# One branch per pair on TensorE, a merged last routing group, and work of the expert stage moved in its queues

## The chip, the cores and the metric

The kernel runs on one core of one Trainium2 chip. The metric is the device time of one execution in microseconds (us), as the median of several runs. PE is TensorE's matmul, PEld its weight load, DVE VectorE, ACT ScalarE, POOL GpSimd, SP SyncE (it issues most of the DMAs). A q behind an engine's name means its sequencer, which waits, loads registers and branches.

## The reference

Random-feature attention, followed by a mixture of experts with one expert per token:

```python
def phi(x):
    proj = np.einsum('bhsd,md->bhsm', x, omega)
    sq = np.sum(x * x, axis=-1, keepdims=True) / 2.0
    h = proj - sq
    h = h - np.max(h, axis=-1, keepdims=True)
    return np.exp(h) / np.sqrt(m)
...
kv = np.einsum('bhsm,bhsd->bhmd', k_p, v)
z = np.sum(k_p, axis=2)
num = np.einsum('bhsm,bhmd->bhsd', q_p, kv)
den = np.einsum('bhsm,bhm->bhs', q_p, z)[..., None] + 1e-06
...
logits = x @ w_gate
expert_idx = np.argmax(logits, axis=1)
...
    h = np.maximum(xe @ w1[e], 0.0)
    ye = h @ w2[e]
    out[mask] = gate_w[mask, None] * ye
```

q, k and v are 8 x 8 x 576 x 64 float32, omega is 128 x 64. The 4608 tokens have 512 columns; there are 8 experts, w1 is 8 x 512 x 1024 and w2 is 8 x 1024 x 512. The expert of a token is known only once its row of the attention is.

## The kernel before, in words

**Attention.** `Attention.run` goes through 72 units (a batch's remainder rows, then its eight heads), a software pipeline written out by hand: in each round of the loop the next unit is transposed, this one projected, the one before exponentiated, and so on, and each engine takes its instructions in just the order in which the code issues them. `unit_sum` adds up k' over the rows on POOL (tile `ks`), and two units later `unit_df` multiplies it on PE. `finish` writes a batch's rows to DRAM (`token_rows`).

**Routing.** While attention runs, `Routing.some` pops small steps from a queue in between. `rest` queues a group of steps (`group`): the argmax of a token's logits, its one-hot row `OH`, its rank among the tokens of its expert (`rr`, many short matmuls), the gate weight. Batches 0 to 5 are grouped in pairs (9 columns), batch 6 and batch 7 alone (4 and 5 columns). For every column two 128 x 128 tiles `rt_RH` are made (`rh`, L600): those that are queued go to POOL a few per round (`row`), those of the last group are the "tail" that `slots` makes, four of them on ACT in two steps each and the rest on DVE. `slots` then counts the tokens of each expert, and one matmul over all `rt_RH` gives the list of tokens in expert order, cut in tiles of 128 (`idx`). `plan` turns the counts into flags that the engines load into registers.

**Experts.** Two tiles of 128 tokens make a pair. Weights and activations are split in a high and a low float32r part, and each product is three matmuls (L990 to L992). Pair 0 is an exception: it is chosen from the first four batches alone, gathered in the last rounds of the attention (`ahead`), and multiplied in plain float32 (`products0`, `l20`), so that PE has work while `slots` runs. From pair 1 on a pair goes so: `gather` (POOL, indirect DMA), `move` (SP: rows to DRAM and back into `xq`, blocked), `xtrans` (DVE: two stream transposes and the low part `xb`; ACT: the high part), `two` (PE: 96 matmuls of layer 1, L927; ACT `relu`, DVE `hlow`), `l2` (PE: 24 matmuls for each of the two tiles), `store`. A pair whose second tile is empty takes `one` in place of `two`, and its second `l2` is skipped: two branches per pair on PE, both by the flag in row 4, `If(full)` in `step` and `when` for `l2(t, 1)`. `change` splits new weights (`split`, L46 on DVE and L52 on ACT) where the expert changes.

The order in a step is the code's: `step(t)` issues the gather of t+2, layer 1 of t, then `following` (that is `begin(t + 1)`: `xtrans(t + 1)`, `move(t + 2)`, the split of new w1), then layer 2 of t, then its branch for the second tile. For this data the expert stage has pairs 1 to 19; two of them have one tile, and both are followed by a change of expert.

```python
    def begin(self, t):
        self.xtrans(t)
        if t + 1 < NPR:
            self.move(t + 1)
        self.change(t, 1)
```

The tiles of `slots` (`f_cnt` and on) come from a pool that opens after the attention and lies on memory that the attention's tiles held.

## Time and profile before

| | us |
|---|---|
| median of 3 runs | 708.39 (707.14 to 709.19) |
| the profiled execution | 707.54 |
| its span, first to last instruction | 705.8 |
| PE busy in the span | 677.3 (96%) |
| PEld / DVE / ACT / POOL busy | 610.2 / 373.2 / 356.6 / 269.0 |
| mean granted clock of TensorE | 0.990 |

The page shows PE busy in nearly every slice, attention to about 246 us, the list of slots to 262 us, then the experts to 692 us. Where one engine is busy throughout, the time follows from the work on that engine and from the few places in which it stands still; these are found in the order of time, engine by engine. Column "idle before" of a timeline row, in brackets, says how long the engine stood still before it and what ended that.

### The profile page before, as it was taken

The numbers are of one execution on the slowest core, as the hardware profiler recorded it, in microseconds if no ns is written. First come the engines' busy times: TensorE is split into PE (matmuls) and PEld (weight loads), VectorE is DVE, ScalarE is ACT, GpSimd is POOL, SyncE is SP. The second block draws the span as 40 slices with busy tenths as digits, with TensorE's granted clock in tenths as the row PEclk, the third lists the DMA queues.
The fourth block names the chain that finished last, engine by engine and source line by source line (L and its number), as shares of the span: only waits on it lengthen the run. The fifth ranks groups of instructions, "written<-read, shape, count | busy, mean of one in ns | idle before, by whom it ended". The sixth has DMA issues, their size and how long they took to land. (4 is left out here: it accounts for less than half of the span.)

```text
span 705.8 us, 19757 instructions
## 1 busy us (share of the span) xinstructions
PE 677.3 (96%) x7590; PEld 610.2 (86%) x7590; DVE 373.2 (53%) x748; ACT 356.6 (51%) x1083; POOL 269.0 (38%) x487
## 2 busy tenths in 40 slices
PE   6999999999999899999999999999999999999992
PEld 5999999999899885999889998899888889998891
DVE  4788888888888776531233272331493376312310
ACT  4999999999999624421222162221272244212210
POOL 5544557877887663212202213112222023122010
PEclk9999999999999999999999999999999999999997
DMA  6872754826672124843223256323257338331200
GB/s 180 245 239 73 233 161 120 266 77 199 214 283 72 33 70 175 253 143 122 76 80 106 92 173 237 107 69 113 91 182 236 102 107 319 109 108 61 77 19 20
DMA packets 92430, 99.56 MB, mean 141 GB/s; under 512 B 28942, under 2 KB 72974, under 8 KB 91664
## 3 DMA queue, kind: packets, MB, share of 16 engines
q1 hardware_dynamic: 85744, 78.91, 35.3%
q0 software_dynamic: 6560, 19.03, 8.0%
q8 instruction: 72, 1.18, 0.7%
q14 instruction: 54, 0.44, 0.2%
HBM read 71.06 MB, written 29.51 MB: 142 GB/s over the span
## 5 line engine op out<-in xcount | busy, mean ns | idle before, releaser
L927 PEld LDWEIGHTS p<-xb,w1p 128*128 128x128 f32 x1632 | 194.7, 188 | 5.7 <-ACT w1p L52 2.9
L927 PE MATMUL p<-xb,w1p 128*128 128x256 f32 x1632 | 196.6, 280 | 2.3 <-ACT w1p L52 2.0
L998 POOL DMA_INDIRECT out_dram<-ys,idx x38 | 41.0, 1080 | 323.2 <-ACT ys L997 206.4
L983 DVE SCALAR_TENSOR_TENSOR hl<-p,hh 128x512 fp32r<-128x512 f32 x68 | 46.5, 691 | 220.5 <-ACT hh L979 210.3
L990 PE MATMUL p<-w2p,hh 128*128 128x512 f32 x288 | 113.9, 396 | 0.0
L991 PE MATMUL p<-w2p,hh 128*128 128x512 f32 x288 | 113.8, 395 | 0.0
L992 PE MATMUL p<-w2p,hl 128*128 128x512 f32 x288 | 113.8, 395 | 0.0
L979 ACT ACTIVATE hh<-p 128x512 fp32r<-128x512 f32 x68 | 40.3, 597 | 127.7 <-PE p L927 123.6
L997 ACT ACTIVATE ys<-p,gt 128x512 f32<-128x512 f32 x38 | 26.2, 688 | 116.8 <-PE p L992 93.4
L172 DVE TENSOR_REDUCE mx<-pp 128x8 f32<-128x1024 f32 x64 | 78.0, 1219 | 9.4 <-PE pp L166 8.7
L180 ACT ACTIVATE qp<-pp,mx 128x128 f32<-128x128 f32 x256 | 76.8, 431 | 0.0
L180 ACT ACTIVATE kp<-pp,mx 128x128 f32<-128x128 f32 x256 | 73.7, 381 | 4.3 <-DVE de L264 1.3
L166 PE MATMUL pp<-omt,th 64*128 64x128 f32 x1024 | 72.1, 281 | 0.0
L992 PEld LDWEIGHTS p<-w2p,hl 128*128 128x128 f32 x288 | 54.1, 188 | 13.2
L991 PEld LDWEIGHTS p<-w2p,hh 128*128 128x128 f32 x288 | 54.1, 188 | 12.2
L990 PEld LDWEIGHTS p<-w2p,hh 128*128 128x128 f32 x288 | 54.1, 188 | 12.2
L166 PEld LDWEIGHTS pp<-omt,th 64*128 64x128 f32 x1024 | 63.5, 191 | 0.0
L192 POOL TENSOR_TENSOR k<-kp 128x256 f32<-128x256 f32 x64 | 46.5, 726 | 26.1 <-ACT kp L180 21.4
L255 PE MATMUL nu<-kva,qt 128*64 128x73 f32 x1008 | 46.6, 235 | 0.0
L157 DVE COPY th<-tr 128x512 f32<-128x512 f32 x63 | 43.3, 687 | 6.1 <-PE tr L151 4.2
L224 ACT COPY qt<-t 128x512 f32<-128x512 f32 x64 | 41.6, 650 | 2.6 <-PE t L151 2.2
L255 PEld LDWEIGHTS nu<-kva,qt 128*64 128x64 f32 x1008 | 37.1, 137 | 4.2
(379 smaller groups left out, 1063.0 us busy)
## 6 DMA issues: line engine op xcount, KB each, us to landing
w1s<-in_moe_w_dram SPq DMA_DIRECT2D x5, 2048.0 KB
w2s<-in_moe_w_dram SPq DMA_DIRECT2D x5, 2048.0 KB
xq<-pair_rows SPq DMA_DIRECT2D x76, 128.0 KB
v<-in_v_dram SPq DMA_DIRECT2D x32, 256.0 KB
token_rows<-x SPq DMA_DIRECT2D x8, 1024.0 KB
k<-in_k_dram SPq DMA_DIRECT2D x31, 256.0 KB
q<-in_q_dram SPq DMA_DIRECT2D x31, 256.0 KB
pair_rows<-xg SPq DMA_DIRECT2D x10, 512.0 KB
```

What stands on the lines that cost most here:

```text
L157: self.nc.vector.tensor_copy(t.rearrange("p n (a t) -> p a n t", a=2), s[("tr", h)])
L166: nc.tensor.matmul(o[:, a, n, :], t[r, n, :], self.om[r], start=True, stop=True)
L172: self.nc.vector.tensor_reduce(out=mx, in_=s[("pp", h)], axis=AX.X, op=ALU.max, negate=True)
L180: self.nc.scalar.activation(o[:, j, :], p[:, a, 2 * n + i, :], AF.Exp, bias=mx[:, a, 2 * n + i:2 * n + i + 1])
L192: nc.gpsimd.tensor_tensor(out=k2, in0=kp[:, :2, :], in1=kp[:, 2:, :], op=ALU.add)
L224: self.nc.scalar.copy(qt.rearrange("p n (a t) -> p a n t", a=2), s[("t2", h)])
L255: nc.tensor.matmul(o[r, j, :], qt[:, j, r], kva[:, h if h >= 0 else 2 * j + a, :], start=True, stop=True)
L927: return [lambda w=w, x=x, c=c, n=n: self.nc.tensor.matmul(o, w[:, c, f], x[:, c, :], start=n == 0, stop=n == len(ops) - 1) for n, (w, x, ...
L983: self.nc.vector.scalar_tensor_tensor(out=b, in0=self.p_1[g], scalar=0.0, in1=a.bitcast(F32), op0=ALU.max, op1=ALU.subtract)
L990: nc.tensor.matmul(p, h[:, c, k], self.w2h[:, c, :], start=c == 0, stop=False)
L991: nc.tensor.matmul(p, h[:, c, k], self.w2l[:, c, :], start=False, stop=False)
L992: nc.tensor.matmul(p, l[:, c, k], self.w2h[:, c, :], start=False, stop=c == self.NF - 1)
```

## The change

It does the following things, which are independent in the code:

- The last two batches form one routing group of 9 columns (`rest`), and its tail of 18 tiles `rt_RH` is dealt out to DVE (10), ACT (4, in two steps each) and POOL (4). `row` is not called in the last two rounds more than before, and the second gather of pair 0 moves from round -3 to round -2.
- The tiles of `slots` and the second gather buffer `xgm` come from pools that live from the start; `xgm` is cleared at the start instead of after the attention.
- Only the first tile of pair 0 has its layer 2 in plain float32. The second is split (`relu0`, `low0`) and multiplied by three float32r matmuls per chunk in step 1 (`l21`), once w2 has been split.
- `plan` and the load of the next w1 come later, the gather of pair 2 earlier.
- In a step, `xtrans(t + 1)` moves from behind layer 1 to before it, `l2(t, 1)` goes into the branch of `two`, before `l2(t, 0)`, and the second branch is left to ACT and POOL. In `one`, a copy moves from DVE to ACT.

```diff
-            if i < n - 1:
+            if i < n - 3:
                 self.routing.row(2 if i % 4 == 0 else 1, self.nc.gpsimd)
...
-        if b > B - 3:
-            self.queue += self.group([b], g, slice(o * NJ, (o + 1) * NJ + o), both)
-        elif o:
+        if o:
             self.queue += self.group([b - 1, b], g, slice(0, GT), both)
...
-            self.tail = r
+            self.tail = [(f, nc.vector if i % 2 == 0 or i == 17 else nc.scalar if i < 8 else nc.gpsimd)
+                         for i, f in enumerate(r)]
...
-    def slots(self, wk, banks, idx, fill):
+    def slots(self, banks, idx, fill):
...
-        t = self.t = lambda n, sh, dt=F32: wk.tile(sh, dt, name="f_" + n)
+        t = self.t = lambda n, sh, dt=F32: self.cp.tile(sh, dt, name="f_" + n)
...
-        self.xg = [cp.tile([P, 2, ROW], F32, name="xg")]
-        self.nc.gpsimd.memset(self.xg[0], 0.0)
+        self.xg = [cp.tile([P, 2, ROW], F32, name=n) for n in ("xg", "xgm")]
+        for x in self.xg:
+            self.nc.gpsimd.memset(x, 0.0)
...
-        if k in (-4, -3):
-            a = k + 4
+        if k in (-4, -2):
+            a = (k + 4) // 2
...
+    def low0(self, g):
+        o, f = self.p_1[g].rearrange("p (f t) -> p f t", t=self.T2), slice(2 * g, 2 * g + 2)
+        self.nc.vector.scalar_tensor_tensor(out=self.hl[0][:, f, :P], in0=o[:, :, P:], scalar=0.0,
+                                            in1=self.hl[0][:, f, P:].bitcast(F32), op0=ALU.max, op1=ALU.subtract)
...
+    def l21(self):
+        p = self.p_2[0]
         for c in range(self.NF):
...
+            self.triple(p, self.hl[0][:, c, P:], self.hl[0][:, c, :P], c)
+        self.store(1, p, self.idx0)
...
-        nc.vector.tensor_copy(f, p[:, :, 1])
+        nc.scalar.copy(f, p[:, :, 1])
...
     def begin(self, t):
 
-        self.xtrans(t)
         if t + 1 < NPR:
             self.move(t + 1)
         self.change(t, 1)
...
     def step(self, t, following):
         if 1 < t < NPR - 2:
             self.gather(t + 2)
+        if 1 < t < NPR - 1:
+            self.xtrans(t + 1)
         if t == 1:
             self.two(t)
+            self.xtrans(2)
+            self.l21()
+            self.when(self.reg(4, t, 1, (ET.PE,)), lambda: self.l2(t, 1))
         else:
             with self.tc.If(self.reg(4, t, 1, (ET.PE, ET.Activation, ET.DVE)) > 0) as full:
                 self.two(t)
+                self.l2(t, 1)
             with full.Else():
                 self.one(t)
         if t == 1:
             self.gather(3)
             self.next(0, 2)
+        if t + 1 < NPR:
+            self.weigh(t + 1)
         following()
         self.l2(t, 0)
-        self.when(self.reg(4, t, 1, (ET.PE, ET.Activation, ET.Pool)), lambda: self.l2(t, 1))
+        self.when(self.reg(4, t, 1, (ET.Activation, ET.Pool)), lambda: self.out2(t, 1))
+        self.out2(t, 0)
...
-        rt.slots(cp, (self.p_2[0], self.p_2[1][:, :256], self.p_2[1][:, 256:]), self.idx, lambda: self.fill(16))
+        rt.slots((self.p_2[0], self.p_2[1][:, :256], self.p_2[1][:, 256:]), self.idx, lambda: self.fill(16))
         self.fill(32)
         self.gather(1)
+        self.gather(2)
+        for g in range(2):
+            self.relu0(g)
+        self.split(1, range(4))
+        for g in range(2, 4):
+            self.relu0(g)
         for g in range(4):
-            self.relu0(g)
-        rt.plan(self.flags)
-        self.split(1)
-        self.next(0, 1)
-        self.l20(0)
+            self.low0(g)
+        self.split(1, range(4, 8))
+        self.l20(range(5))
...
+        self.weigh(1)
+        self.l20(range(5, NF))
+        self.store(0, self.p_2[1], self.idx0)
         self.move(2)
+        rt.plan(self.flags)
+        self.next(0, 1)
```

Where the instructions stand now, at three places. First PE in pair 2 of the experts, from the last two matmuls of the first of the two layer 2 products on (`p_6280` is tile 0, `p_6281` tile 1; L990 to L992 is `l2`, L1003 is `when`). Before:

```order
L991 MATMUL p_6280<-w2p_6285,hh_6296 128x512
L992 MATMUL p_6280<-w2p_6284,hl_6298 128x512
L874 TENSOR_LOAD flags
L874 ISA x2
L1003 COMPARE_AND_BRANCH
L990 MATMUL p_6281<-w2p_6284,hh_6296 128x512
```

and now, from the last matmul of `l2(2, 0)` (`p_6246`) to the first of the next pair's layer 1 (L943):

```order
L868 MATMUL p_6246<-w2p_6250,hl_6262 128x512
L891 TENSOR_LOAD flags
L891 ISA x2
L1019 UNCONDITIONAL_BRANCH
L1049 COMPARE_AND_BRANCH
L943 MATMUL p_6465<-xb_6258,w1p_6248 128x256
```

The register load and the branch ahead of the second tile's product are gone; what stands between two pairs is the load and the branch of `If(full)` alone.

Second, DVE around a one-tile pair (L956 to L959 is `hid_one`, L910 the stream transposes, L46 the splits). Before, the end of `one`, then the next pair's rows, then the split of new w1:

```order
L959 SCALAR_TENSOR_TENSOR hl_6298<-hs_6292,hh_6296 128x2x128
L1029 UNCONDITIONAL_BRANCH
L910 STREAM_TRANSPOSE xgm<-xq 128x512 x2
L46 TENSOR_TENSOR xb_6294<-xgm,xb_6294 128x4x128 x2
```

and now, the rows of the next pair, then this pair's branch, `hlow` or `hid_one`, then the split of new w1:

```order
L927 STREAM_TRANSPOSE xgm<-xq 128x512 x2
L46 TENSOR_TENSOR xb_6258<-xgm,xb_6258 128x4x128 x2
L891 TENSOR_LOAD flags
L1049 COMPARE_AND_BRANCH
...
L975 SCALAR_TENSOR_TENSOR hl_6262<-hs_6256,hh_6260 128x2x128
L1049 UNCONDITIONAL_BRANCH
L891 TENSOR_LOAD flags
L1019 COMPARE_AND_BRANCH
L46 TENSOR_TENSOR w1p_6249<-w1s,w1p_6248 128x512 x8
```

The transposes and `xb` of the next pair left the place between `hid_one` and the split of w1.

Third, POOL in the last rounds of the attention (L192 to L194 is `unit_sum`, the DMA at L808 the gather of pair 0, L609 the tiles `rt_RH`). Before:

```order
L194 TENSOR_TENSOR ks_5_5908<-ks_5_5908,kp_-1_5315 64x128
L808 DMA xg<-token_rows,idx_78 128x520
L591 COPY ga_5926<-se_5903 128x32
L275 TENSOR_TENSOR lg_4579<-lg_4579,lh_3_5986 128x32
L609 TENSOR_SCALAR rt_RH<-rt_iob,rt_RM,rt_ilo 128x128
L192 TENSOR_TENSOR k_7_6_5991<-kp_6_5977 128x256
L193 TENSOR_TENSOR ks_6_5992<-k_7_6_5991 128x128
L194 TENSOR_TENSOR ks_6_5992<-ks_6_5992,kp_-1_5315 64x128
```

and now:

```order
L194 TENSOR_TENSOR ks_5_5875<-ks_5_5875,kp_-1_5317 64x128
L275 TENSOR_TENSOR lg_4581<-lg_4581,lh_3_5947 128x32
L192 TENSOR_TENSOR k_7_6_5951<-kp_6_5938 128x256
L193 TENSOR_TENSOR ks_6_5952<-k_7_6_5951 128x128
L194 TENSOR_TENSOR ks_6_5952<-ks_6_5952,kp_-1_5317 64x128
L808 DMA xg<-token_rows,idx_78 128x520
```

The gather stands behind the sums of head 6, and the copy `ga` and one `rt_RH` are gone from before them.

## Rows read from the trace of the kernel before

**Rows 1.** Timeline of PE, two pairs: start, length, instruction [idle before].

```profile
302.11 11.47 PE L927 MATMUL p<-xb,w1p 128*128 128x256 f32 x96
313.41 0.40 PE L990 MATMUL p<-w2p,hh 128*128 128x512 f32 x1
...
324.62 0.28 PE L927 MATMUL p<-xb,w1p 128*128 128x256 f32 x1
```

**Rows 2.** Timeline of PE at the two one-tile pairs' ends.

```profile
517.39 0.39 PE L992 MATMUL p<-w2p,hl 128*128 128x512 f32 x1
518.79 12.15 PE L927 MATMUL p<-xb,w1p 128*128 128x256 f32 x96 [1.00 <-ACT w1p L52]
...
578.60 12.39 PE L927 MATMUL p<-xb,w1p 128*128 128x256 f32 x96 [1.00 <-ACT w1p L52]
```

**Rows 3.** Timeline of PE, last rounds of the attention.

```profile
240.65 0.28 PE L236 MATMUL kf<-one,ks 128*64 128x1 f32 x4 [1.62 <-POOL ks L194]
...
244.73 0.75 PE L816 MATMUL x_turn<-ident,xg 128*128 128x128 f32 x4
```

**Rows 4.** Busy time by stretch, PE alone: stretch, length, busy, PEclk (granted clock), DMA.

```profile
241.00:245.00 4.00, 4.00 (x60) 0.57 0.00 0
```

**Rows 5.** Timeline of POOL at the same place.

```profile
236.40 1.12 POOL L808 DMA_INDIRECT xg<-token_rows,idx  x1 [0.28 <-POOL ks L194]
...
237.98 0.80 POOL L609 TENSOR_SCALAR rt_RH<-rt_iob,rt_RM,rt_ilo 128x128 bf16<-128x128 bf16 x1
...
240.09 0.51 POOL L194 TENSOR_TENSOR ks<-ks,kp_-1_5315 64x128 f32<-64x128 f32 x1
```

**Rows 6.** Transfers issued from 230 to 250 us: count, median us from issue to landing.

```profile
xg<-token_rows,idx POOLq DMA_INDIRECT x2, 3.6
```

**Rows 7.** Timeline of DVE in the slots.

```profile
255.37 0.17 DVE L704 TENSOR_SCALAR f_cnt<-p 128x8 f32<-128x8 f32 x1 [1.64 <-DMA token_rows<-xr]
...
260.01 1.20 DVE L609 TENSOR_SCALAR rt_RH<-rt_iob,rt_RM,rt_ihi 128x128 bf16<-128x128 bf16 x5
```

**Rows 8.** Timeline of PE, layer 2 of pair 0, first tile, and what follows.

```profile
264.91 7.03 PE L850 MATMUL p<-w2s,h 128*128 128x512 f32 x16
271.77 0.64 PE L816 MATMUL p_1tr<-ident,xgm 128*128 128x128 f32 x4
```

**Rows 9.** PE's sequencer, 514 to 519 us, by line: count, durations in ns, first and last start.

```profile
L874 PEldq TENSOR_LOAD <-flags x2: 305/366/427, 514.1 to 518.0; - x2
...
L1003 PEldq EVENT_SEMAPHORE  x1: 51/51/51, 517.8 to 517.8; - x1
```

**Rows 10.** Timeline of DVE behind the first one-tile pair.

```profile
513.99 2.11 DVE L910 STREAM_TRANSPOSE xg<-xq 128x512 f32<-128x512 f32 x2
516.11 1.41 DVE L46 TENSOR_TENSOR xb<-xg,xb 128x512 fp32r<-128x512 f32 x2
517.63 4.91 DVE L46 TENSOR_TENSOR w1p<-w1s,w1p 128x512 fp32r<-128x512 f32 x8
```

**Rows 11.** Timeline of SP, two moves begun, and of DVE where it waits for the first.

```profile
283.98 0.38 SPq L901 DMA_DIRECT2D pair_rows<-xg  x1
...
354.51 0.38 SPq L901 DMA_DIRECT2D pair_rows<-xg  x1
...
294.32 2.09 DVE L910 STREAM_TRANSPOSE xg<-xq 128x512 f32<-128x512 f32 x2 [1.89 <-DMA xq<-pair_rows]
```

**Rows 12.** Timeline of POOL and PE at the start.

```profile
0.96 0.96 POOL L789 MEMSET xg<- 128x1040 f32 x1
...
7.95 1.06 POOL L95 MEMSET rv<- 128x256 f32 x4
...
14.19 0.34 PE L151 MATMUL tr<-ident,q 64*128 64x64 f32 x4 [0.26 <-DMA q<-in_q_dram]
```

**Rows 13.** Two branches of PE's sequencer, 501 us and 688 us: durations in ns.

```profile
L1029 PEldq COMPARE_BRANCH  x1: 356/356/356, 501.5 to 501.5; - x1
...
L1047 PEldq COMPARE_BRANCH  x1: 3328/3328/3328, 688.1 to 688.1; - x1
```

More of the change, by code (lines that the diff above doesn't have):

```diff
@@ L520, in group @@
         bc = lambda a: a.unsqueeze(2).to_broadcast([P, n, E])
-        t = lambda nm, sh: (self.cp.tile(sh, F32, name=f"l_{nm}") if last else
+        t = lambda nm, sh: (self.cp.tile(sh, F32, name=f"l_{nm}") if nm in ("nr", "nl") else
                             wk.tile(sh, F32, name=f"{nm}_{b}", tag="g_" + nm))
@@ L602, in f @@
                 pay = (self.ihi, self.ilo)[k]
-                if last and k and i < 4:
+                if eng is nc.scalar:
                     d = wk.tile([P, P], BF16, name=f"l_d{i}", tag="l_d")
@@ L720, in slots @@
                                     in1=self.iop[:, :NS].unsqueeze(1).to_broadcast([P, GT, NS]), op=ALU.is_equal)
-        for f in self.tail:
-            f(nc.vector)
+        for f, eng in self.tail:
+            f(eng)
         for n, pp in enumerate((pa, pb)):
@@ L844, in relu0, with l20, triple @@
     def relu0(self, g):
-        self.nc.scalar.activation(self.h0[:, 2 * g:2 * g + 2, :].rearrange("p f t -> p (f t)"), self.p_1[g], AF.Relu)
-    def l20(self, a):
-        p = self.p_2[a]
-        for c in range(self.NF):
-            self.nc.tensor.matmul(p, self.h0[:, c, a * P:(a + 1) * P], self.w2s[:, c, :], start=c == 0,
-                                  stop=c == self.NF - 1)
-        self.store(a, p, self.idx0)
+        o, f = self.p_1[g].rearrange("p (f t) -> p f t", t=self.T2), slice(2 * g, 2 * g + 2)
+        self.nc.scalar.activation(self.h0[:, f, :P], o[:, :, :P], AF.Relu)
+        self.nc.scalar.activation(self.hl[0][:, f, P:], o[:, :, P:], AF.Relu)
+    def low0(self, g):
+        o, f = self.p_1[g].rearrange("p (f t) -> p f t", t=self.T2), slice(2 * g, 2 * g + 2)
+        self.nc.vector.scalar_tensor_tensor(out=self.hl[0][:, f, :P], in0=o[:, :, P:], scalar=0.0,
+                                            in1=self.hl[0][:, f, P:].bitcast(F32), op0=ALU.max, op1=ALU.subtract)
+    def l20(self, cs):
+        for c in cs:
+            self.nc.tensor.matmul(self.p_2[1], self.h0[:, c, :P], self.w2s[:, c, :], start=c == 0, stop=c == self.NF - 1)
+    def l21(self):
+        p = self.p_2[0]
+        for c in range(self.NF):
+            self.triple(p, self.hl[0][:, c, P:], self.hl[0][:, c, :P], c)
+        self.store(1, p, self.idx0)
+    def triple(self, p, h, l, c):
+        for x, w in ((h, self.w2h), (h, self.w2l), (l, self.w2h)):
+            self.nc.tensor.matmul(p, x, w[:, c, :], start=c == 0 and x is h and w is self.w2h,
+                                  stop=c == self.NF - 1 and x is l)
     def fill(self, n):
@@ L917, in parts @@
             split_r(self.nc, self.xh[t % 2][:, :, s], self.xl[t % 2][:, :, s], x[a], self.nc.scalar, self.nc.vector)
-        self.weigh(t)
     def products(self, t, g, b):
@@ L986, in l2, with out2 @@
     def l2(self, t, a):
-        nc, i, k = self.nc, 2 * t + a, slice(a * P, (a + 1) * P)
+        nc, k = self.nc, slice(a * P, (a + 1) * P)
         h, l, p = self.hh[t % 2], self.hl[t % 2], self.p_2[a]
         for c in range(self.NF):
-            nc.tensor.matmul(p, h[:, c, k], self.w2h[:, c, :], start=c == 0, stop=False)
-            nc.tensor.matmul(p, h[:, c, k], self.w2l[:, c, :], start=False, stop=False)
-            nc.tensor.matmul(p, l[:, c, k], self.w2h[:, c, :], start=False, stop=c == self.NF - 1)
-        self.store(i, p, self.idx)
+            self.triple(p, h[:, c, k], l[:, c, k], c)
+    def out2(self, t, a):
+        self.store(2 * t + a, self.p_2[a], self.idx)
     def store(self, i, p, idx):
@@ L1058, in run @@
         self.ys = ring("ys", [P, DM], F32, 3)
-        self.xg.append(cp.tile([P, 2, ROW], F32, name="xgm"))
-        nc.gpsimd.memset(self.xg[1], 0.0)
         self.hs = ring("hs", [P, 2, P], F32, 2)
@@ L1080, in run @@
         self.parts(1, [self.turn(self.xg[1][:, a], self.bank(g)) for a, g in enumerate(("tr", "t2"))])
-        self.gather(2)
-        self.l20(1)
+        self.weigh(1)
+        self.l20(range(5, NF))
+        self.store(0, self.p_2[1], self.idx0)
         self.move(2)
+        rt.plan(self.flags)
+        self.next(0, 1)
         for t in range(1, NPL - 1):
```

## The prediction

> **What bounds the kernel now.** I read the page first: PE is busy for 677.3 of the 705.8 us, so the time is PE's work plus the places where PE stands still or runs slower than it could. Then PE's timeline from end to end, and at each hole the timeline of whoever ended it.
>
> In the experts a full pair takes 324.62 - 302.11 = 22.51 us [rows 1]: layer 1 from 302.11 to 313.41, then 48 matmuls at (324.62 - 313.41)/48 = 0.2335 us. No row there has an idle time in brackets: in full pairs PE is the bound, and the second branch is passed by a sequencer that runs ahead. The two pairs with one tile end differently [rows 2]: the next layer 1 starts 1.4 us after the last matmul has started, instead of 0.23, and takes 12.15 and 12.39 us instead of 11.47.
>
> Late in the attention PE waits 1.62 us for the sums `ks` [rows 3], and in the 4 us that follow the granted clock is 0.57 [rows 4], mostly the lower of its two levels (1.2 instead of 2.4 GHz). In the slots DVE waits 1.64 us ahead of `f_cnt`, put down to the transfer of `xr` to `token_rows` [rows 7], on which no count of tokens depends: what the tile waits for is its memory.
>
> **The change part by part.** All against the profiled execution, 707.54 us, which lies 0.85 below the median of the runs shown.
>
> *Expert stage, full pairs: 0.* PE has the same 144 matmuls. A register load and a branch go from a place where they were covered.
>
> *After one-tile pairs: -3.9.* The hole is (518.79 - 517.39) - 0.23 = 1.17 us, the same (1.15) at the second, and layer 1 is 0.68 and 0.92 longer: 3.9 in all. Two things cause it, one behind the other. PE's sequencer, which otherwise runs about 3 us ahead, reaches the skipped branch with an EVENT_SEMAPHORE at 517.8, when PE's last matmul is just done, and loads the next flag only at 518.0 [rows 9]. And DVE has the transposes (2.11) and `xb` (1.41) of the next pair ahead of the split of w1, which starts at 517.63 and takes 4.91 us [rows 10], eight pieces at 0.61: its first piece is there at 518.2, and layer 1 then eats pieces about as fast as they come, hence the longer layer 1. The change takes the first away (no skipped branch on PE) and moves the 3.5 us of the second ahead of this pair's layer 1, so that the split starts near 514. I take the whole: -3.9. With only the branch gone the split still binds and some 0.8 is gained; with only the split earlier, the hole stays and 1.6 is gained.
>
> *Loop end: -3.0.* Ahead of the sums that end at 240.60, POOL does the second gather (1.12) and an `rt_RH` (0.80), and the copy `ga` [rows 5]; all of them leave, 2.1 us with the copy's estimated 0.2. That is more than the wait of 1.62, which goes. If PE is not stopped there, I expect no fall of the clock behind it either: 4.00 x (1 - 0.57) = 1.72 us. Together -3.34. Next late is the gathered tile: the gather starts after the sums, near 238.5, and lands 3.6 us after its issue [rows 6], near 242.1; its transposes on PE stand at 244.73 [rows 3], 3.34 earlier at 241.4. Some of those 0.7 us are covered by products next to it, so I take half back, -3.0. From nothing gained behind the wait itself (-1.6) to all and a little of batch 6's grouping that leaves the loop (-3.9).
>
> *Slots: -0.5.* The tiles of `slots` lie in memory of their own now, so DVE's 1.64 us goes. Against it DVE makes ten `rt_RH` where six stood, at 1.20/5 = 0.24 [rows 7]: +0.96. POOL's four tiles at 0.80 and ACT's run beside that. The group's small operations grow from 5 to 9 columns and PE has eight more short products: +0.2. Bounds: -1.2 if the larger group hides part of it, +0.2 if the wait was half somebody else's.
>
> *Second tile of pair 0: -1.3.* One tile's plain layer 2 lasts from 264.91 to 271.77, 6.86 us [rows 8]; by three float32r matmuls per chunk it is 24 x 0.2335 = 5.60. The splits of it are eight short operations on ACT and four on DVE, under PE's first tile. The split of w2 has a pair's layer 1, 11.3 us, before it is wanted. If it is late, up to the whole 1.3 is lost.
>
> *Start: +0.6.* Clearing `xgm` costs POOL 0.96 and now stands with `xg`'s, ahead of clearing `rv` [rows 12]. The loads of `rv` wait for that on SP, and the later loads of q and k queue behind them. PE already waits 0.26 for a q at 14.19, so there is no slack at the end of this chain, and about 0.4 in front of SP. Between 0 and 1.0; I take 0.6.
>
> *Transposes before `hlow`: 0.* `xtrans(t + 1)` now stands on DVE ahead of what finishes the current pair's hidden layer. If its rows are late, the current pair waits, where before only the next one did. A move starts 354.51 - 347.13 = 7.4 us into a pair (302.11 + 2 x 22.51 = 347.13), and the slowest seen took 294.32 - 283.98 = 10.3 us [rows 11]. So rows are there 17.7 us into the previous pair, and with 3.5 us of DVE at 21.2; they are wanted at 22.5 + 11.3 = 33.8. Twelve us to spare; less where weights change and in the first pairs, where `xtrans(3)` has some 3.
>
> Sum: -3.9 - 3.0 - 0.5 - 1.3 + 0.6 = -8.1, so 699.4 where the profiled run had 707.5. Against the median I add half of its 0.85: **699.8**.
>
> **A rule that speaks against it.** PE's branch into a far place is not free here: entering the one-tile path took 356 ns, hidden since it came at 501.5 for a matmul at 504.67; the one out of the loop at 688.1 took 3328 ns [rows 13]. The second tile's 24 matmuls lie inside the pair's branch now, so that one-tile pairs jump further. The Trainium skill (Runtime: NRT & Kernel Launch, Instruction fetch mechanics) says that a taken branch to a target outside the prefetched window stalls until that page is fetched. The 3328 ns agree with such a stall. By it, both one-tile pairs could pay that on entering (a rival below); without it the sum stands.
>
> **Rivals.**
> *One cause stays.* One-tile pairs still stop PE, for the sequencer or for the split: between 0.8 and 1.6 of 3.9 gained, 699.8 + 3.9 - 1.6 = 702.1, or 702.9. For it: two causes stood in one place, and a third (ACT's half of the split, which the row names) may be behind them. Against: ACT loses its half of `xtrans` there too.
> *Longer jump.* Entering the one-tile path costs as much as the far branch did, 3.33 us, against a lead of 504.67 - 501.5 = 3.17: 0.16 of hole each, +0.3, 700.1. Against: the two paths stand only 24 matmuls further apart.
> *The loop still stops.* PE waits for the gathered tile instead of `ks`, the clock falls there, and nothing of the 3.0 is gained; with half of the one-tile gain lost too, about 705. For it: the gather is later than before by about 2 us and lands 0.7 behind its wish. Against: other heads' products stand around it.
> *DVE in order, a little.* In pair 2 and where weights change the rows come late and `hlow` waits: +2, 702.
> *DVE in order, everywhere: slower.* If moves beside the loads of weights take longer than the seen 10.3 us, every full pair stops before layer 2. That begins at 10.3 + 12 = 22.3 us; from there each us costs each of 17 full pairs one. The 8.1 us are eaten at 0.5 us per pair, so from 22.8 us on the kernel is slower; at 23.5 us it would be 699.8 + 17 x 1.2 = 720. For it: one move did hold DVE up by 1.89 us. Against: that was the first, and later ones held nobody.
>
> **How the numbers follow.** Forecast 0.70; one cause stays 0.12; DVE a little 0.06; longer jump 0.04; the loop still stops 0.04; slower 0.04. The forecast's own bounds: all good ends (-3.9, -1.2 in the slots, 0 at the start) give 696.9, all bad ones of loop, slots and w2 some 703. The range is 696.5 to 703.5; it leaves out the slower case, the loop's, and tails. A change of 0.3% (2.1 us) is about what a measurement of this kernel can tell from none. All cases but the slower one lie under 708.39 - 2.1 = 706.3; 0.05 is left for two or three misses that come together: faster 0.91, same 0.05, slower 0.04.
>
> **What would show it.** Right: no wait for `ks` on PE near 240 us and a granted clock near 1.0 in the 4 us behind it; `f_cnt` straight behind the group's operations; 24 float32r matmuls of 5.6 us for pair 0's second tile behind pair 1's layer 1; after one-tile pairs no idle time on PE and layer 1 at 11.5; PE's wait for q at 14 us longer by half a us. Wrong: a pair of more than 22.51 us, with DVE's transposes waiting for `xq` and PE's layer 2 for `hl`, or a new wait of PE for `xg` at the loop's end with the clock at one half behind it.

## The result, and the profile after

The changed kernel takes 700.34 us (median of 5 runs, 699.37 to 701.15) against 708.52 for the kernel before beside it (5 runs, 707.14 to 710.42): a ratio of 0.9883, 95% interval 0.9865 to 0.9901. The forecast was 699.8 in 696.5 to 703.5. The profiled execution took 701.15 us, its span is 699.3.

The time between the same places of both traces (starts of PE's instructions; `nu` is the product at L255, the first of 72 groups):

| stretch | before | after | difference | predicted |
|---|---|---|---|---|
| span's start to first `nu` | 21.35 | 23.60 | +2.25 | +0.6 |
| to pair 0's first product (L840) | 225.22 | 224.72 | -0.50 | -3.0 |
| to pair 0's layer 2 (slots lie in it) | 18.34 | 16.91 | -1.43 | -0.5 |
| to layer 1 of pair 2 | 37.20 | 35.68 | -1.52 | -1.3 |
| to the last matmul's end | 390.11 | 384.58 | -5.53 | -3.9 |
| to the span's end | 13.5 | 13.8 | +0.3 | 0 |

The sum is -6.4, where the medians differ by 8.2: the profiled execution of the kernel before lay 0.85 below its median, that of the changed kernel is the slowest of its five. Only some of the lines are near the forecast's. The page's PE line first (busy time, share, instructions):

```profile
PE 672.8 (96%) x7596; PEld 615.6 (88%) x7596; DVE 372.6 (53%) x738; ACT 359.9 (51%) x1096; POOL 272.4 (39%) x484
```

PE's timeline of one full pair answers to [rows 1], and what follows the two one-tile pairs to [rows 2]:

```profile
300.91 11.68 PE L943 MATMUL p<-xb,w1p 128*128 128x256 f32 x96
312.42 0.63 PE L868 MATMUL p<-w2p,hh 128*128 128x512 f32 x2
323.33 0.88 PE L943 MATMUL p<-xb,w1p 128*128 128x256 f32 x6
...
515.31 0.39 PE L868 MATMUL p<-w2p,hl 128*128 128x512 f32 x1
515.54 11.68 PE L943 MATMUL p<-xb,w1p 128*128 128x256 f32 x96
...
573.01 0.39 PE L868 MATMUL p<-w2p,hl 128*128 128x512 f32 x1
573.23 11.68 PE L943 MATMUL p<-xb,w1p 128*128 128x256 f32 x96
```

No row has an idle time in brackets: the stop of 1.17 us and the longer layer 1 behind one-tile pairs are gone. But a full pair is not what it was. Layer 1 takes 312.42 - 300.91 = 11.51 us where it took 11.30, and layer 2 323.33 - 312.42 = 10.91 where it took 11.20, with the same matmuls. Nothing in the prediction speaks of that.

The loop's end, PE's timeline, then PE by stretch (length, busy, PEclk, DMA), which answer to [rows 3, 4]:

```profile
246.27 0.28 PE L236 MATMUL kf<-one,ks 128*64 128x1 f32 x4 [1.53 <-POOL ks L194]
```

```profile
240.00:245.00 5.00, 4.54 (x86) 1.00 0.19 54
245.00:250.00 5.00, 3.73 (x48) 1.00 0.01 4
```

The wait for `ks` did not go. It moved by one head, from head 6 to head 7, and is 1.53 us long where it was 1.62. In this profile no lower clock follows it. POOL's timeline says why the wait is there (against [rows 5]):

```profile
241.56 0.45 POOL L194 TENSOR_TENSOR ks<-ks,kp_-1_5317 64x128 f32<-64x128 f32 x1
242.28 1.05 POOL L808 DMA_INDIRECT xg<-token_rows,idx  x1 [0.27 <-issue]
...
245.76 0.45 POOL L194 TENSOR_TENSOR ks<-ks,kp_-1_5317 64x128 f32<-64x128 f32 x1 [0.87 <-DMA xg<-token_rows,idx]
```

POOL's last addition of head 7 stands still until the gather has landed, and starts 3.5 us after the gather did. The first gather does the same to head 5's, which waits 0.94 us at 239.47, but PE does not notice that. In the traces POOL's sequencer has a semaphore wait for the outstanding gathers ahead of the additions of odd heads (their rows lie in the upper 64 partitions) and none ahead of those of even ones; what puts it into the program was not found. In the kernel before, the second gather stood ahead of head 6, and head 7's addition came when it had long landed.

In the slots DVE's wait ahead of `f_cnt` is gone ([rows 7]); nine of the ten `rt_RH` now take 2.09 us:

```profile
253.93 0.15 DVE L703 TENSOR_SCALAR f_cnt<-p 128x8 f32<-128x8 f32 x1
...
258.99 2.09 DVE L607 TENSOR_SCALAR rt_RH<-rt_iob,rt_RM,rt_ihi 128x128 bf16<-128x128 bf16 x9
```

Pair 0's second tile has its 24 matmuls behind pair 1's layer 1, 5.46 us from the first one's start to the start of what follows (the length in the row counts the last one to its end):

```profile
284.56 5.63 PE L868 MATMUL p<-w2p,hl 128*128 128x512 f32 x24
```

And the start. PE waits 0.36 us for q instead of 0.26 [rows 12], and then the same sixteen `pp` products take 2.02 us, which took 1.11 in the kernel before:

```profile
14.61 0.48 PE L151 MATMUL tr<-ident,q 64*128 64x64 f32 x4 [0.36 <-DMA q<-in_q_dram]
14.88 2.02 PE L166 MATMUL pp<-omt,th 64*128 64x128 f32 x16
```

### The profile page after: what moved, and what is told of

Read it like the earlier page. It is cut to its first block, busy times and chain, and to the rows that moved or that the text cites. A ratio compares the mean times of both kernels' runs of the same rounds, so it can differ in the third digit from the quotient of the medians.

```text
span 699.3 us, 19723 instructions
## 1 busy us (share of the span) xinstructions
PE 672.8 (96%) x7596; PEld 615.6 (88%) x7596; DVE 372.6 (53%) x738; ACT 359.9 (51%) x1096; POOL 272.4 (39%) x484
## 5 line engine op out<-in xcount | busy, mean ns | idle before, releaser
L943 PEld LDWEIGHTS p<-xb,w1p 128*128 128x128 f32 x1632 | 198.1, 192 | 1.7 <-issue 0.5
L943 PE MATMUL p<-xb,w1p 128*128 128x256 f32 x1632 | 198.9, 283 | 0.0
L868 PE MATMUL p<-w2p,hh 128*128 128x512 f32 x576 | 177.8, 390 | 0.0
L1014 POOL DMA_INDIRECT out_dram<-ys,idx x38 | 39.4, 1038 | 313.4 <-ACT ys L1013 201.3
L868 PE MATMUL p<-w2p,hl 128*128 128x512 f32 x312 | 117.7, 389 | 0.0
L868 PEld LDWEIGHTS p<-w2p,hl 128*128 128x128 f32 x312 | 58.5, 188 | 12.2
L192 POOL TENSOR_TENSOR k<-kp 128x256 f32<-128x256 f32 x64 | 46.6, 728 | 27.7 <-ACT kp L180 21.8
L927 DVE STREAM_TRANSPOSE xgm<-xq 128x512 f32<-128x512 f32 x18 | 18.9, 1086 | 51.3 <-DMA xq<-pair_rows 51.3
L255 PE MATMUL nu<-kva,qt 128*64 128x73 f32 x1008 | 46.0, 233 | 0.0
L255 PEld LDWEIGHTS nu<-kva,qt 128*64 128x64 f32 x1008 | 36.7, 136 | 4.2
L206 PE MATMUL kf<-kp,v 128*64 128x128 f32 x512 | 39.4, 275 | 0.0
```

The source lines that it names most:

```text
L192: nc.gpsimd.tensor_tensor(out=k2, in0=kp[:, :2, :], in1=kp[:, 2:, :], op=ALU.add)
L206: nc.tensor.matmul(pkv[c * D:(c + 1) * D, :M], vv, kk, start=n < 2, stop=n > 2)
L255: nc.tensor.matmul(o[r, j, :], qt[:, j, r], kva[:, h if h >= 0 else 2 * j + a, :], start=True, stop=True)
L868: self.nc.tensor.matmul(p, x, w[:, c, :], start=c == 0 and x is h and w is self.w2h, stop=c == self.NF - 1 and x is l)
L943: return [lambda w=w, x=x, c=c, n=n: self.nc.tensor.matmul(o, w[:, c, f], x[:, c, :], start=n == 0, stop=n == len(ops) - 1) for n, (w, x, ...
```

## The experiments

All are the changed kernel with the edit shown, timed beside the kernel before, and profiled. Four things were open: the start's 2.25 us, the wait at the loop's end, what the hole behind one-tile pairs was made of, and the new pace of PE in the experts.

**1. The start: xgm cleared in the loop.**

```diff
-        for x in self.xg:
-            self.nc.gpsimd.memset(x, 0.0)
+        self.nc.gpsimd.memset(self.xg[0], 0.0)
...
+        if k == -60:
+            nc.gpsimd.memset(self.xg[1], 0.0)
```

> The changed kernel with one thing undone at the start: xgm is cleared during the attention loop, not at the start. Theory A (the clearing of xgm holds rv's and then k's and q's loads up, and PE, which waits longer for them, stays at the lower pace until 20 us): the 16 products of the first pp after 14 us take 1.1 us again instead of 2.0, the first nu comes at about 21.4 us instead of 23.6, and the whole is 2.0 to 2.7 us faster than the changed kernel's 700.3, near 698. Theory B (the two profiled executions differ at the start by chance, the first q rows landed 0.4 us later in one of them): at most 0.6 us, near 700, and the first nu's place differs from profile to profile.

Measured: 698.71 us (4 runs), ratio 0.9856 [0.9837, 0.9875]. PE's timeline of this run, and below it that of run 3, which clears `xgm` at the start as the changed kernel does:

```profile
14.68 2.02 PE L166 MATMUL pp<-omt,th 64*128 64x128 f32 x16
```

```profile
14.59 1.11 PE L166 MATMUL pp<-omt,th 64*128 64x128 f32 x16
```

Without the clearing the slow products are there (first `nu` at 22.58), with it they are not (21.57). The time alone would not have settled it: 698.71 lies between the two forecasts, and 0.5 to 0.9 us under runs 2 and 3, which were timed beside it with the clearing at the start. The traces speak for theory B: PE's pace up to 20 us differs between profiled executions, whatever the clearing does. In the twelve runs the first `nu` starts between 21.57 and 23.89 us. Those that have `xgm` cleared at the start and their products fast at 14 us are 0.2 to 0.45 later than the kernel before (21.57, 21.70, 21.71, 21.79 against 21.35): that is the clearing's price, and the rest of the 2.25 was not seen to be the change's. From the first `nu` on to the last rounds there are such differences too (201.4 to 203.4 us up to the ninth last group). These come at three places, with up to 0.6, 1.2 and 0.9 us. So the loop's end is compared from the ninth last group to the fifth last (the expectations' "head 7 - 4"), 13.27 us before and 12.26 after, and from there to pair 0's first product, 10.56 before and 9.44 after.

**2. The loop's end: the second gather back in round -3.**

```diff
-        if k in (-4, -2):
-            a = (k + 4) // 2
+        if k in (-4, -3):
+            a = k + 4
```

> The changed kernel with the second gather of pair 0 back in round -3, between the sums of heads 5 and 6. Theory A (POOL's sum of an odd head waits for the gather's landing, 3.5 us after its issue, and the changed kernel put the gather right in front of such a sum): PE's wait of 1.53 us for ks of head 7 goes; in its place PE waits up to 1 us for ks of head 6, because the gather's 1.1 us are ahead of it again, without the copy and rt_RH of before; net 0.5 to 1.5 us faster than the changed kernel, 698.8 to 699.8. Theory B (POOL is simply full there): the wait comes back at head 6 with its 1.6 us and the lower clock behind it, 1 to 2 us slower, 701.5 to 702.5.

Measured: 699.59 us (4 runs), 0.9873 [0.9856, 0.9891], not to be told from the changed kernel. The trace tells more. PE's timeline, and PE by stretch:

```profile
240.76 0.28 PE L236 MATMUL kf<-one,ks 128*64 128x1 f32 x4 [1.36 <-POOL ks L194]
```

```profile
240.00:245.00 5.00, 4.24 (x63) 0.66 0.05 20
```

Head 7's wait is gone, as theory A has it, but the wait is back at head 6, with the lower clock behind it, and from the fifth last group of `nu` to pair 0's first product it takes 10.54 us. With the `rt_RH` and the copy gone from POOL the wait is only 0.26 shorter than before the change. That is not because they were worth little: counted from the ninth last group, the sum of head 6 ends 1.1 us earlier (16.8 instead of 17.9), but PE, whose work up to there has shrunk too, comes 0.8 us earlier to its wait for it. The loss of 1 to 2 us that theory B expected did not come.

**3. The pace: all of the experts' tiles 32 bytes further.**

```diff
         cp = ctx.enter_context(self.tc.tile_pool(name="mo_c", bufs=1))
+        cp.tile([P, 8], F32, name="pad")
```

> The changed kernel with an unused tile of 32 bytes per partition ahead of the experts' tiles, so that all of them lie 32 bytes further, as they did modulo 64 before the change; nothing else. Theory A (the place of the operands in memory sets the pace of the matmuls: a full pair's layer 1 went from 11.30 to 11.51 us and its layer 2 from 11.20 to 10.91 with the change): layer 1 at 11.30 and layer 2 at 11.20 again, a pair 22.51 instead of 22.42, 17 pairs x 0.09 = 1.5 us slower, 701.8. Theory B (the pace belongs to the order of the instructions, l2 of the second tile inside the branch): 11.51 and 10.91 as in the changed kernel, same time.

Measured: 699.25 us (4 runs), 0.9872 [0.9855, 0.9888]; layer 1 310.63 - 299.12 = 11.51, layer 2 321.54 - 310.63 = 10.91 us. Nothing moved: where all the tiles start, modulo 64, is not it. The order of the instructions is then left, or the distance between tiles. Run 5 below, which puts a part of the old order back, leaves the pace at 11.51 and 10.91.

```profile
299.12 11.68 PE L943 MATMUL p<-xb,w1p 128*128 128x256 f32 x96
310.63 0.63 PE L868 MATMUL p<-w2p,hh 128*128 128x512 f32 x2
321.54 0.64 PE L943 MATMUL p<-xb,w1p 128*128 128x256 f32 x4
```

**4 and 5. The hole behind one-tile pairs: each of the two edits undone alone.** First `xtrans` behind layer 1 again:

```diff
     def begin(self, t):
 
+        if t > 2:
+            self.xtrans(t)
...
-        if 1 < t < NPR - 1:
-            self.xtrans(t + 1)
```

> The changed kernel with xtrans(t + 1) behind layer 1 again, so that after a one-tile pair the transposes stand ahead of the split of new w1 on DVE; the second tile's layer 2 stays in the branch. Theory A (two causes in series, as the prediction has it: the sequencer's stop is gone, the late split remains): after one-tile pairs PE waits about 0.7 us for w1p and layer 1 is 0.7 to 0.9 longer; 3.1 of the 3.9 us come back, near 703.4. Theory B (the sequencer's stop was all of it): no wait, 700.3. Theory C (the late split alone was all of it, the sequencer's stop lay beside it): all 3.9 come back, 704.2.

Then the second tile's layer 2 out of the branch again:

```diff
                 self.two(t)
-                self.l2(t, 1)
...
         self.l2(t, 0)
+        if t > 1:
+            self.when(self.reg(4, t, 1, (ET.PE,)), lambda: self.l2(t, 1))
```

> The changed kernel with the second tile's layer 2 on PE taken out of the branch of two and put behind the first tile's, under a branch of its own, as before; xtrans stays ahead of layer 1, so the split of w1 is early. It is the other half of the run that put xtrans back, in which layer 1 after a one-tile pair took 13.3 us instead of 11.5 with no stop ahead of it. Theory A (the skipped branch stops PE's sequencer by itself): the stop of 1.17 us behind each of the two one-tile pairs is back, layer 1 stays 11.5 us; 2 x 1.2 = 2.3 us slower than the changed kernel. Theory B (the stop was only the wait for the split): no stop, same time. The pace (layer 1 at 11.51, layer 2 at 10.91): if it belongs to the place of the instructions, 11.30 and 11.20 come back here; if to the place of the operands, it stays.

Measured: 704.95 us (6 runs, 0.9944 [0.9925, 0.9962]) and 706.53 (12 runs, 0.9978 [0.9968, 0.9989]). PE's and DVE's timelines with `xtrans` back:

```profile
516.34 0.39 PE L943 MATMUL p<-xb,w1p 128*128 128x256 f32 x1
517.07 12.75 PE L943 MATMUL p<-xb,w1p 128*128 128x256 f32 x95 [0.34 <-DVE w1p L46]
529.65 0.63 PE L868 MATMUL p<-w2p,hh 128*128 128x512 f32 x2
```

```profile
512.78 2.06 DVE L927 STREAM_TRANSPOSE xg<-xq 128x512 f32<-128x512 f32 x2
...
516.32 4.91 DVE L46 TENSOR_TENSOR w1p<-w1s,w1p 128x512 fp32r<-128x512 f32 x8
```

PE's timeline with the branch back, and its sequencer's row (durations in ns, start):

```profile
514.39 0.39 PE L868 MATMUL p<-w2p,hl 128*128 128x512 f32 x1
516.06 11.77 PE L943 MATMUL p<-xb,w1p 128*128 128x256 f32 x96 [1.28 <-ACTq L1019]
```

```profile
L1019 PEldq EVENT_SEMAPHORE  x1: 51/51/51, 514.8 to 514.8; - x1
```

With the split late (it starts at 516.32; at 512.90 in the changed kernel), the first matmul of layer 1 starts at once, the second waits for DVE's first piece, and layer 1 takes 529.65 - 516.34 = 13.31 us instead of 11.51, at both places: 3.6 us in all. ACT's half of the split moves with the same edit, so DVE's half and ACT's are not told apart. With the branch back and the split early, PE stops 516.06 - 514.39 - 0.23 = 1.44 us, the sequencer waiting until PE is empty as before, and layer 1 is 0.1 longer: 3.1 in all. Both at once cost 3.9 before the change. So they lie beside each other and don't add up: to undo either one takes back most of what both together give. (The median of the first run is 4.6 us above the changed kernel's; its trace shows nothing beyond the 3.6 in the expert stage, but the clock fell at the loop's end. The rest of the 6.2 us of the second run lies at the very end, 17.0 us from the last matmul to the span's end instead of 13.8: in it the stores of the last pair both wait for its last matmul.)

**6, 11 and 12. The pace: the distance of the operands.** The change took `xgm` (4160 bytes per partition) away from between the split weights and the activations. The first pad is 64 bytes between split w1 and w2; the second stands behind w2; the third is the first with 1024 bytes. The distances in the table are worked out from the order and the sizes of the tiles in the code.

```diff
-        (self.w1h, self.w1l), (self.w2h, self.w2l) = (ring(n, [P, c, w], F32R, 2) for n, c, w in
-                                                      (("w1p", NC, F), ("w2p", NF, DM)))
+        self.w1h, self.w1l = ring("w1p", [P, NC, F], F32R, 2)
+        cp.tile([P, 16], F32, name="pad")
+        self.w2h, self.w2l = ring("w2p", [P, NF, DM], F32R, 2)
```

> The changed kernel with an unused tile of 64 bytes per partition between the two buffers of split w1 and those of split w2. In the kernel before, xb lay 19 x 4096 + 64 bytes behind w1p and hh 15 x 4096 + 64 behind w2p; in the changed kernel both distances are whole multiples of 4096 (18 and 14). With the pad xb is 64 off w1p again, and hh is still a whole multiple off w2p. Theory A (the distance between the two operands of a matmul sets its pace): layer 1 at 11.30 us as before the change, layer 2 at 10.91 as after it, a full pair at 22.21, some 17 x 0.21 + 2 = 3.7 us faster than the changed kernel, 696.6. Theory B (the pace has nothing to do with the distance): 11.51 and 10.91, same time as the changed kernel.

> The changed kernel with the 64-byte tile behind split w2 instead of between split w1 and split w2: xb is 64 bytes off w1p as in the kernel before, and now hh is 64 off w2p too, as in the kernel before. Theory A (the distance of a matmul's two operands sets its pace, at 64 bytes faster for layer 1 and slower for layer 2): layer 1 at 11.30 us, layer 2 at 11.20, a full pair 22.51 as before the change; 1.6 us slower than the changed kernel, 702, and 5.8 slower than with the pad between. Theory B (only the distance of xb and w1p counts, and layer 2's 10.91 has another cause): 11.30 and 10.91, 696 as with the pad between.

> The changed kernel with a pad of 1024 bytes instead of 64 between split w1 and split w2: xb is 18 x 4096 + 1024 bytes behind w1p, hh a whole multiple of 4096 behind w2p. Theory A (layer 1 is slow only where the distance of its operands is a whole multiple of 4096 bytes): layer 1 at 11.30 us as with 64, some 696. Theory B (what counts is the distance within a smaller unit that divides 1024, so 64 bytes off is another place and 1024 is not): 11.51 us as without a pad, 700. Layer 2 stays at 10.9 in both.

PE's timeline of a full pair, with 64 bytes ahead of w2, with 64 behind w2, and with 1024 ahead of w2:

```profile
297.10 11.47 PE L943 MATMUL p<-xb,w1p 128*128 128x256 f32 x96
308.41 0.63 PE L868 MATMUL p<-w2p,hh 128*128 128x512 f32 x2
319.30 0.87 PE L943 MATMUL p<-xb,w1p 128*128 128x256 f32 x6
```

```profile
301.57 11.47 PE L943 MATMUL p<-xb,w1p 128*128 128x256 f32 x96
312.88 0.63 PE L868 MATMUL p<-w2p,hh 128*128 128x512 f32 x2
324.08 1.10 PE L943 MATMUL p<-xb,w1p 128*128 128x256 f32 x8
```

```profile
298.69 11.68 PE L943 MATMUL p<-xb,w1p 128*128 128x256 f32 x96
310.20 0.63 PE L868 MATMUL p<-w2p,hh 128*128 128x512 f32 x2
321.11 1.12 PE L943 MATMUL p<-xb,w1p 128*128 128x256 f32 x8
```

| kernel | xb behind w1p, beyond a multiple of 4096 | layer 1 | hh behind w2p, likewise | layer 2 | time, ratio |
|---|---|---|---|---|---|
| before | 64 | 11.30 | 64 | 11.20 | |
| changed | 0 | 11.51 | 0 | 10.91 | 700.34, 0.9883 |
| all by 32 | 0 | 11.51 | 0 | 10.91 | 699.25, 0.9872 |
| 64 ahead of w2 | 64 | 11.31 | 0 | 10.89 | 696.04, 0.9833 [0.9819, 0.9848] |
| 64 behind w2 | 64 | 11.31 | 64 | 11.20 | 703.37, 0.9927 [0.9908, 0.9946] |
| 1024 ahead of w2 | 1024 | 11.51 | 0 | 10.91 | 699.65, 0.9877 [0.9848, 0.9907] |

Theory A of the first two: the two layers follow the distances, each its own, and in opposite directions: layer 1 is quicker with 64, layer 2 with 0. For layer 2 the distance is told apart from the place of either operand: `hh` lies in the same place with 64 ahead of w2 and with 64 behind it, `w2p` in the same place with 64 behind it and in the changed kernel, and the pace differs in both comparisons. For layer 1 it is not quite: in these runs `w1p` never moved without `xb`, so the place of `xb` alone is not excluded. Of the 3.0 us by which the run with 64 behind w2 is slower than the changed kernel, 1.6 lie in pairs 2 to 19, as expected; in its profile the clock also fell at the loop's end.

Theory B of the third: 1024 is like 0. That says less than it seems. The pieces of the tiles that single matmuls read lie whole multiples of 512 bytes apart, so layer 1 has matmuls at every such distance, whatever multiple of 512 the tiles are moved by. In the changed kernel all 96 of them go alike, 0.12 us from start to start from the second on: multiples of 512 all count as 0. Which smaller unit counts, and how the reads collide, was not tried. The whole change's 0.087 us per full pair is this, and came by accident.

**7, 9 and 10. The loop's end: both gathers earlier.** In rounds -5 and -4:

```diff
-        if k in (-4, -2):
-            a = (k + 4) // 2
+        if k in (-5, -4):
+            a = k + 5
```

> The changed kernel with both gathers of pair 0 one and two rounds earlier, in rounds -5 and -4, so that neither stands near the sums of heads 6 and 7 on POOL. Theory A (the wait for ks at the loop's end is the gather, by its 1.1 us on POOL or by its landing): no wait of PE for ks of heads 6 and 7, no lower clock behind it; from the products of head 7 - 4 on to pair 0's first product 9.4 us become 7.9 or less; 1.5 us faster than the changed kernel, up to 2.7 where that showed the lower clock. Theory B (POOL is late for other reasons): the wait moves to an earlier head, no gain.

Measured: 698.76 us (4 runs), 0.9858 [0.9841, 0.9875], the same as the changed kernel. PE's and POOL's timelines:

```profile
239.47 0.28 PE L236 MATMUL kf<-one,ks 128*64 128x1 f32 x4 [0.50 <-POOL ks L194]
...
241.55 0.28 PE L236 MATMUL kf<-one,ks 128*64 128x1 f32 x4 [0.45 <-POOL ks L194]
```

```profile
238.97 0.45 POOL L194 TENSOR_TENSOR ks<-ks,kp_-1_5317 64x128 f32<-64x128 f32 x1 [1.05 <-DMA xg<-token_rows,idx]
```

Head 7 waits no more, but head 5's addition now stands behind the gather of round -4, and PE meets that lateness twice, 0.95 us together; the granted clock of 240 to 245 us was 0.69, and the stretch from the fifth last `nu` took 10.12 us. So the gather is in front of an odd head again. Both in round -5, behind head 3, would land ahead of head 5. The run with that, run 10, has the pad of 64 bytes and the clearings in the loop too, to make the best version, and run 9 is the same with the gathers where the changed kernel has them. Run 10's gathers:

```diff
-        if k in (-4, -2):
-            a = (k + 4) // 2
+        for a in range(2 if k == -5 else 0):
```

> The changed kernel with the 64-byte tile between split w1 and split w2, and with both clearings (xg and xgm) in the attention loop. Theory (the two add up): the pad gives its 4.2 us (a full pair at 22.19); the clearings gone from POOL's start let the later loads of k and q go up to 1.9 us earlier, so PE's waits for k and q at 14 us shrink by up to 0.5 and with them the chance of the lower pace up to 20 us: 694 to 696. Rival (the start is set by the landing of the first k and q and by chance): no gain beside the pad's, 696.0.

> As the run before, and both gathers of pair 0 in round -5, one behind the other, behind the sum of head 3. Theory A (what makes POOL late in the last rounds is the wait of an odd head's sum for the landing of a gather; with the gathers in rounds -5 and -4 that was head 5's, 1.05 us): both have landed by then, no wait of PE for ks above 0.3 us, the granted clock stays 1.00 from 235 to 250 us, and from the products of head 7 - 4 on to pair 0's first product 9.4 us become 7.9 or less: 1.5 us faster than the run before. Theory B (POOL has too much to do in these rounds, wherever the gathers stand): waits of 0.5 us and more stay, and no gain.

Measured: 694.98 us (0.9820 [0.9802, 0.9838]) without, 692.61 (0.9782 [0.9766, 0.9799]) with the gathers in round -5, 5 runs each. The clearings in the loop gave nothing that can be told from run 6 (696.04); the gathers 2.4 us. The only row of PE's timeline from 225 to 268 us with an idle time, and PE by stretch, of the last:

```profile
235.74 0.28 PE L236 MATMUL kf<-one,ks 128*64 128x1 f32 x4 [0.25 <-POOL ks L194]
```

```profile
240.00:245.00 5.00, 5.00 (x104) 1.00 0.00 0
245.00:250.00 5.00, 5.00 (x46) 1.00 0.52 198
```

From the fifth last `nu` to pair 0's first product it takes 7.30 us, where it was 10.56 before the change and 9.44 after; the four groups before that take 12.74 instead of 12.26, since the two gathers now delay head 4's sum, for which PE waits 0.25. Theory A: POOL has the same work in both runs, and with the gathers elsewhere the waits are gone. How much of a wait is the landing (0.87 us in POOL's row of head 7) and how much the gather's own time on POOL (1.05) this run does not separate. This is the quickest version found, 7.7 us under the changed kernel by the medians, 7.2 by the two ratios.

**8. The slots: their tiles back in the pool that opens late.**

```diff
-    def slots(self, banks, idx, fill):
+    def slots(self, wk, banks, idx, fill):
...
-        t = self.t = lambda n, sh, dt=F32: self.cp.tile(sh, dt, name="f_" + n)
+        t = self.t = lambda n, sh, dt=F32: wk.tile(sh, dt, name="f_" + n)
...
-        rt.slots((self.p_2[0], self.p_2[1][:, :256], self.p_2[1][:, 256:]), self.idx, lambda: self.fill(16))
+        rt.slots(cp, (self.p_2[0], self.p_2[1][:, :256], self.p_2[1][:, 256:]), self.idx, lambda: self.fill(16))
```

> The changed kernel with the tiles of slots in the pool that opens after the attention, as before the change. Theory A (their memory is what DVE waited for ahead of f_cnt): DVE waits 1.5 us or more for a transfer of the attention ahead of f_cnt again, and from pair 0's first product to the first of its layer 2, 16.9 us become 18.0 to 18.6; 1.1 to 1.7 us slower. Theory B (the gain in this stretch came from the larger group and the tiles dealt out to POOL and ACT): the stretch stays at 16.9.

Measured: 702.99 us (6 runs), 0.9922 [0.9907, 0.9936]: 2.65 slower than the changed kernel. DVE's and PE's timelines:

```profile
255.32 0.17 DVE L703 TENSOR_SCALAR f_cnt<-p 128x8 f32<-128x8 f32 x1 [1.82 <-DMA token_rows<-xr]
```

```profile
260.25 2.90 PE L724 MATMUL p<-f_T,rt_RH 128*128 128x50 bf16 x45 [0.38 <-DVE rt_RH L607]
262.99 4.52 PE L840 MATMUL p<-x,w1s 128*128 128x256 f32 x12
```

Theory A, and more than expected: the stretch takes 21.06 us instead of 16.91. DVE's wait is back, PE stops twice for a moment, and the twelve plain products behind that take 4.52 us where they take 2.84 in the changed kernel: the granted clock from 260 to 265 and from 265 to 270 us was 0.84 and 0.82. So the late tiles cost their wait, and in this profile a fall of the clock on top; the latter is some 1.7 of the 4.15 us, estimated as 5.00 x (1 - 0.84) + 5.00 x (1 - 0.82). How many of the six executions had it is not known.

## Why the prediction was right, point by point

The time lay within the range and 0.5 us off the forecast. Part of that is luck. The parts as measured below add up to about -9.9 us and not to -8.1: the loop's end gained 0.9 less than forecast, the slots 0.9 more, and the new pace, which was not foreseen, another 1.6. Against that the profile of the changed kernel holds some 3.5 us of slower stretches ahead of the loop's end (1.9 at the start, 1.6 from there to the ninth last group) that were not seen to be the change's, so that the two traces differ by 6.4 us only. The medians differ by 8.2; how much of such stretches is in them no run shows.

- *Full pairs, 0: wrong in size.* The count of matmuls was right and the branch was covered, but a pair is 22.42 us and not 22.51. The step that failed is "PE has the same 144 matmuls", taken as the same time. The pace of a matmul hung on where its operands lie, and moving `xgm` to a lasting pool moved them (runs 3, 6, 11, 12). For the fourteen full pairs from pair 2 on that do not follow a one-tile pair it gave -1.2 us.
- *After one-tile pairs, -3.9: right in sum, wrong in structure.* The one-tile pairs, 11 and 14, and the pairs behind them took 74.85 us together before and 70.54 after: 4.31 less, of which 0.4 is the pace. But the prediction had two causes "one behind the other", 0.8 for the branch alone and 1.6 for the split alone. Runs 4 and 5 put back 3.6 and 3.1 of the 3.9: so the branch edit alone would have gained some 0.3 (forecast 0.8), the earlier split alone some 0.8 (forecast 1.6). The order of the waits on one engine had been read as a sum, where the two ran side by side.
- *Loop end, -3.0: mis-sized, by a wait that was not seen.* That the wait of head 6 would go was right, and so was that the gather is late next; that PE would stand before the gathered tile's transposes was wrong, and "no wait for `ks`", the prediction's own sign of being right, did not come. That the lower clock stayed away is true of this profile, but not of every one with this wait (last section). The gather held POOL for 1.05 us by itself and for 0.87 by its landing, a wait ahead of head 7's addition, and PE's wait came back nearly whole: -1.1 us from the fifth last `nu` on, and -1.0 in the four groups before that, which have no steps of batch 6's group now (the likely reason; no run took it alone): -2.1 instead of -3.0. The row that showed such a wait ([0.15 <-DMA xg<-token_rows,idx] ahead of an odd head's sum) was in the trace of before, and small.
- *Slots, -0.5: mis-sized, -1.43.* That the memory was worth a good part is shown (run 8): 2.65 us by the medians, more than the 1.64 that DVE waited, though part of it can be the lower clock that run 8's profile has. The price of the larger group can't be told apart from that. The stretch takes 16.90 us in eight profiles with this code, and up to 18.34 in those in which the clock fell (run 3).
- *Second tile of pair 0, -1.3: right.* 5.46 us of matmuls for 6.86, -1.4; with the new pace of pair 1 the stretch came to -1.52.
- *Start, +0.6: right in sign, smaller.* 0.2 to 0.45 (run 1); the other 1.8 of this profile come and go between executions.
- *Transposes before `hlow`, 0: right.* In no pair does PE wait ahead of layer 2. DVE's transposes do wait for `xq`, 14 times and 76.3 us together; the longest wait, 16.30 us, ends in pair 2, where the first `hlow` starts behind them only at 309.24 and PE still gets its layer 2 at 312.42 without a stop.

Of the rivals, the longer jump of PE's branch did not show: PE enters both one-tile pairs without idle time, and the sequencer's branches there took 364 and 439 ns, where they took 356 and 331 before. The rule of the Trainium skill behind it (Runtime: NRT & Kernel Launch, Instruction fetch mechanics: a branch out of the prefetched window stalls) is thus neither borne out nor refuted here, since the 24 more matmuls cost nothing that PE could see. The rival of the loop that still stops was half right: it stops, though for `ks` and not for the gathered tile, and its clock did not fall in this profile. In the prediction's range, the good ends that it names add up to 697.6 and not to 696.9; nothing hangs on it.

## What to carry to other kernels

Two waits that end at about the same time look like a chain on the engine's row; take one away alone, in thought and on the chip, before you add their prices up. When tiles are moved to another pool, compare the time of one matmul in the untouched inner loop before and after: 0.002 us per matmul of layer 1 was worth some 4 us of 700 here, and a pad of 64 bytes got it. And an asynchronous transfer has a price at its landing as well as at its issue: look in the order for who waits for it next on the engine that issued it.

## What the runs showed of the hardware that I had not expected

- The pace of float32r matmuls depends on how far apart their operands' tiles lie in a partition. With 64 bytes beyond a multiple of 4096, the 128x256 matmuls of layer 1 start 0.1177 us apart, with 0 or 1024 beyond it 0.1199. For the 128x512 matmuls of layer 2 it is 0.2333 with 64 and 0.2273 with 0. The two layers prefer opposite places. They differ in shape, but also in which operand lies behind: in layer 1 the moving one (`xb`), in layer 2 the one that is loaded as weights (`hh`). Which of the two makes the difference was not tried.
- A stop of PE of 1.4 to 1.6 us at head 7 had the granted clock fall to 0.66 in a 5 us stretch behind it in some profiles (runs 4, 9, 11; in run 3 to 0.70) and not in others (the changed kernel, runs 1, 5, 6, 8, 12), with the same kernel code around it. What decides was not found; a forecast can only price it as a chance.
- At the start PE ran its products at half pace up to 14 us in some executions and up to 16 to 20 in others (2.02 or 1.11 us for the same sixteen), worth up to 2.3 us. In runs 1, 5, 8 and 12 the profile's granted clock is 0.50 to 0.61 from 16 to 18 us; in the changed kernel and in runs 4, 9, 10 and 11 it says 1.00 over the same half pace. So at the start that column alone did not tell the pace.
